# Attention followed by a SoLU feed-forward: size check, weight conversion, softmax sums and weight check placed differently

## The chip, the cores and the metric

The kernel runs on one core of a Trainium2 chip. The metric is the device time in microseconds of one execution. The times of the kernel before are 870.80, 867.64 and 868.82 us, median 868.82. Names of engines: PE is TensorE (matmuls), PEld its weight loads, DVE is VectorE, ACT is ScalarE, POOL is GpSimd, SP is the engine whose queue issues most transfers.

## The reference, cut to what matters

```python
# attention: q, k, v are (8, 12, 448, 64)
q_n, k_n = rmsnorm(q, g_q), rmsnorm(k, g_k)
scores = q_n @ k_n.T / 8
attn = exp(scores - max) / (sum(exp(scores - max)) + 1e-9)
x = attn @ v                      # then laid out as (3584 tokens, 768)
# feed-forward: w_in (768, 1024), w_out (1024, 768), given as 8-byte floats
h = x @ w_in
u = h * softmax(h)                # over the 1024 columns
ln = (u - mean(u)) / sqrt(var(u) + 1e-6) * g_ln
out = ln @ w_out                  # (3584, 768), float32
```

## The kernel before

The kernel has a fast path and a general one. The fast path computes with number ranges that it checks as it goes: the gains (`gain_limit`), the absolute size of x (`largest`), and the exponents of all weights (`check_w`, `check_all`). At the end one flag says whether the general path must run; with these inputs it doesn't. What follows is the fast path.

**Attention.** The 96 heads go two at a time as a pair `n`, and two pairs make a quad `m`, 24 quads in all. For each pair `scores` makes keys-by-queries blocks, ACT takes their exponentials (`E`, L756), and `values` multiplies them with v. The last 64 keys of both pairs of a quad are handled together (`scores_last`, `values_last`, block number `NJ` = 3). The denominators come from `sums`: matmuls with a matrix of ones over `E` 3 (of the quad), `E` 2 (of each pair), and `es`, which is `E` 0 + `E` 1, added beforehand on DVE by `add` (L789). Each of the three terms takes eight matmuls. `inverse` and `divide` finish the quad, and `store_x` writes it to a DRAM buffer.

**Weights.** Twelve pieces of w_in and sixteen of w_out arrive as raw 64-bit words and are converted by `convert_w` in three steps: `low_bits` (two ACT operations, L521 and L522), `join` (two DVE operations, L527 and L528), and, for w_out, `product` (one ACT operation, L533). Twenty pieces are converted during the quads. The last eight, all of w_out, have their loads issued when the attention's buffers are released after quad 23. `combine` then makes differences of weight blocks on POOL (L548), four for each of the four row blocks c of w_out.

**Feed-forward.** 28 token tiles go two at a time as a group `g`. Each of the two products of a group is computed with seven block products instead of eight (Strassen's scheme in Winograd's form). These need sums of the left operand's blocks, made on POOL by `block_sums`: `xsum` of x for the first product, `us` of the transposed u for the second, two operations for part 0 and two for part 1. `in_parts(g)` is the list of the seven products with w_in, in the order p1, p6, p2, p7, p5, p4, p3; `out_parts(g)` is the same with w_out. After a group's h is there, each tile t goes through `ff_max` (DVE), `ff_exp` (ACT), `ff_mult` (DVE), `ff_moments` (DVE, with a power on POOL at L999), `ff_norm` (DVE) and `ff_spread` (a DVE transpose at L1013 and sixteen small transfers into `uT` at L1020). For tile 0 half of these transfers are issued from ACT's queue.

**What sets the order.** Everything lies in a section with a schedule written by hand: on each engine the instructions run in the order in which the Python code emits them. Each entry of the list `parts` is one unit, one block product. The units are in(0), in(1), in(2), out(0), in(3), out(1) and so on, seven each, and out(12), out(13) at the end. `follow(parts, i, f)` emits f directly after unit i; `later(n, f)` emits f n units on, and things due at the same time come out in the order in which they were registered. For g = 0 and 1 the tile steps come 1, 2, 3, 4, 5 and 6 units after the product that completes h, tile 2g+1 one unit before tile 2g. So the steps of tiles 1 and 0 begin after units 5 and 6, those of tiles 3 and 2 after units 12 and 13. `block_sums` for `xsum` of group 2 come after units 9 and 10, of group 3 after 16 and 17; for `us` of group 0 after 18 and 19. The first product with w_out is unit 21; unit 22 is the first that reads `us`.

The eight late conversions, in the kernel before, are placed by this line:

```python
follow(parts, (1, 2, 2, 3, 4, 4, 5, 6)[i], lambda x=x: convert_next(x))
```

and the sixteen combines of w_out after units 0 to 3, 3 to 6, 8 to 11 and 12 to 15. `largest(g + 1)` comes after the second product of `in_parts(g)`, and for group 0 at the end of quad 22. `check_all` comes after unit 188, before the last seven products. Five PSUM buffers serve the block products, so PE may run up to five units ahead of the DVE operations that consume them (L928).

Of the kernel before, what the change touches and what calls it, by code (L numbers as in the profile page):

```python
# [366 lines left out]
def fast_path(  # L367
# [192 lines left out]
    def check_w(x, raw):  # L560
# [2 lines left out]
        nc.vector.tensor_reduce(extent[:, 0, x : x + 1], hi, AX, OP.min, apply_absolute_value=True)  # L563
        nc.vector.tensor_reduce(extent[:, 1, x : x + 1], hi, AX, OP.max, apply_absolute_value=True)

    def check_all():


        worst = small.tile([P, 3], FP32, tag="worst", name="worst", bufs=1)
        one = small.tile([1, 4], FP32, tag="one", name="one", bufs=1)  # L570
        pw = ps_t.tile([P, 4, P], FP32, tag="t", name="pw")[0:1]
        nc.vector.tensor_reduce(worst[:, 0:1], extent[:, 0], AX, OP.min)
        nc.vector.tensor_reduce(worst[:, 1:2], extent[:, 1], AX, OP.max)
        nc.vector.tensor_reduce(worst[:, 2:3], xmax, AX, OP.max)
        for i in range(3):
            nc.tensor.transpose(pw[:, i], worst[:, i : i + 1], ident)
        nc.vector.tensor_reduce(one[:, 0:1], pw[:, 0], AX, OP.min)
        nc.vector.tensor_reduce(one[:, 1:3], pw[:, 1:3], AX, OP.max)
        nc.vector.tensor_scalar(one[:, 0:1], one[:, 0:1], 2.0 ** -15, None, OP.is_ge)
        nc.vector.tensor_scalar(one[:, 1:2], one[:, 1:2], 2.0, None, OP.is_lt)  # L580
        nc.vector.tensor_scalar(one[:, 2:3], one[:, 2:3], 4.0, None, OP.is_le)
        nc.vector.tensor_tensor(one[:, 0:1], one[:, 0:1], one[:, 1:2], OP.mult)
        nc.vector.tensor_tensor(one[:, 0:1], one[:, 0:1], one[:, 2:3], OP.mult)

        nc.vector.tensor_scalar(one[:, 1:2], large, -1.0, 1.0, OP.mult, OP.add)
        nc.vector.tensor_tensor(one[:, 0:1], one[:, 0:1], one[:, 1:2], OP.mult)
        nc.vector.tensor_scalar(large, one[:, 0:1], -1.0, 1.0, OP.mult, OP.add)
# [195 lines left out]

    def add(n):
        d = st[n]
        d["es"] = work.tile([P, 2, S], FP32, tag="es", name="es")
        nc.vector.tensor_tensor(d["es"], d["E", 0], d["E", 1], OP.add)  # L789

    def values_last(m):

# [22 lines left out]
    def sums(m):  # L815

        d = quads[m]
        sm = d["sm"] = ps_t.tile([P, S], FP32, tag="t", name="sm")
        terms = [
            lambda i: (ones[:, 1 + i], d["E", NJ]),  # L820
            lambda i: (ones[:, 0], st[2 * m + i]["E", 2]),
            lambda i: (ones[:, 0], st[2 * m + i]["es"]),
        ]
        for x, term in enumerate(terms):
            for h in range(2):
                for i in range(2):
# [47 lines left out]
            (nc.sync if g < LAG else nc.scalar).dma_start(x[:, :, o : o + n], xd[b].rearrange("(c p) t -> p c t", p=P)[:, :, c : c + n])  # L874
            t += n

    def largest(g):
        nc.vector.tensor_reduce(
            xmax[:, g : g + 1], gs[g, "x"].rearrange("p c t -> p (c t)"), AX, OP.max, apply_absolute_value=True
        )  # L880

    def x_blocks(g):
        x = gs[g, "x"]
        gs[g, "s"] = xs.tile([P, 3, HD, P], FP32, tag="x", name="xsum")
        return [x[:, i * HD : (i + 1) * HD, k * P : (k + 1) * P] for k in range(2) for i in range(2)]

    def u_blocks(g):
# [17 lines left out]
    def products(g, kind, w, n, c11, c12, c21, c22, done):  # L907


        k = {}  # L910

        def mul(a, i):
            a11, a12, a21, a22 = gs[g, kind]
            sm = gs[g, "s" if kind == "A" else "us"]
            a = {"a11": a11, "a12": a12, "s3": a21, "a22": a22, "s1": sm[:, 0], "s2": sm[:, 1], "s4": sm[:, 2]}[a]
            tag = "tttoo"[len(banks) % 5]
            banks.append(tag)
            o = k["o"] = ps_t.tile([P, 512], FP32, tag=tag, name="b", bufs=3 if tag == "t" else 2)[:, 0:n]
            last = a.shape[1] - 1
            for c in range(last + 1):  # L920
                nc.tensor.matmul(o, a[:, c], w[:, i, c], start=(c == 0), stop=(c == last))  # L921

        def part(name):
            k[name] = second.tile([P, 512], FP32, tag="part", name=name, bufs=4)[:, 0:n]
            return k[name]

        def plus(out, x):
            nc.vector.tensor_tensor(out, k["o"], k[x], OP.add)  # L928

        def p1():  # L930
            mul("a11", 0)
            nc.scalar.copy(part("q1"), k["o"])  # L932

        def p6():
            mul("s2", 5)
            plus(part("u2"), "q1")

        def p2():
            mul("a12", 1)
            plus(c11(), "q1")  # L940
# [83 lines left out]
    def in_parts(g):  # L1024
        def done(i):
            t = 2 * g + i

            units = (1, 2, 3, 5, 7, 9) if g >= LAG else (1, 2, 3, 4, 5, 6)
            for x, f in zip(units, (ff_max, ff_exp, ff_mult, ff_moments, ff_norm, ff_spread)):
                later(x, lambda f=f: f(t))  # L1030

        h = [lambda t=2 * g + k, i=i: half_of(t, "h", DFF // 2, "h", i, 3) for k in range(2) for i in range(2)]
        p = products(g, "A", w_in, DFF // 2, *h, done)
        if g + 2 < NG:
            follow(p, 6, lambda: load_x(g + 2))
        if g + 1 < NG:
            follow(p, 1, lambda: largest(g + 1))
            follow(p, 2, lambda: block_sums(g + 1, "A", 0))
            follow(p, 3, lambda: block_sums(g + 1, "A", 1))
        if g >= LAG:  # L1040
            follow(p, 2 if g > LAG else 4, lambda: block_sums(g - LAG, "U", 0))
            follow(p, 4 if g > LAG else 5, lambda: block_sums(g - LAG, "U", 1))
        return p

    def out_parts(g):
        def done(i):
            t = 2 * g + i
            queue = nc.scalar if t == NT - 2 else nc.sync
            queue.dma_start(out[t * P : (t + 1) * P, :], mt.pop(t)["y"])

        y = [lambda t=2 * g + k, i=i: half_of(t, "y", HO, "y", i, 3) for k in range(2) for i in range(2)]
        p = products(g, "U", w_out, HO, *y, done)
        if NG - LAG <= g + 1 < NG:
            follow(p, 4, lambda: block_sums(g + 1, "U", 0))
            follow(p, 5, lambda: block_sums(g + 1, "U", 1))
        return p

    def follow(p, i, f):
        g = p[i]

        def both():
            g()
            later(1, f)

        p[i] = both
# [25 lines left out]
    xmax = consts.tile([P, NG], FP32, name="xmax")  # L1091
    raws = []
    sets = {}

# [23 lines left out]
    with tc.manual_schedule():  # L1118
# [4 lines left out]
        rsqrt_seed(st[0])  # L1123
        gain_columns()
        rsqrt_step(st[0])
        gain_limit()
        for s in range(2):
            normalise_rows(0, s)
            transpose_rows(0, s)
        take_rows(0, 0)  # L1130
        for s in range(2):
            square_rows(1, s, nc.scalar)
# [5 lines left out]
        for m in range(NQ):  # L1138
# [88 lines left out]
                    load(b + 6)  # L1227
            if m >= NQ // 2:
                combine(w_in, m - NQ // 2)
            unit(lambda: scores(b, 2))  # L1230
            if m == 1:
                qk_transpose(a + 2)
# [14 lines left out]
            if next2:  # L1247
                row_sums(b + 4)
                fold_sums(m + 2)
            unit(outputs)  # L1250
            step(m - 2)
            begin(m)
# [11 lines left out]
                later(1, lambda m=m: divide(m))  # L1264
            if m == NQ - 2:
                load_x(0)
                largest(0)
        divide(NQ - 1)
        store_x(NQ - 1)
        first.close()  # L1270
# [27 lines left out]
            parts += out_parts(NG - LAG + g)  # L1298

        for i, x in enumerate(left):  # L1300
            follow(parts, (1, 2, 2, 3, 4, 4, 5, 6)[i], lambda x=x: convert_next(x))
        for x in range(4 * HF):
            follow(parts, (0, 3, 8, 12)[x // 4] + x % 4, lambda x=x: combine(w_out, x))
        follow(parts, 14, check_first)

        for x in range(len(again)):
            follow(parts, (2 * LAG + 1 + 2 * (x // 3)) * 7 - 7 * LAG + (0, 4, 5)[x % 3], lambda x=x: check_next(x))
        follow(parts, 7 * (2 * NG - 1) - 1, check_all)
        for p in parts:
            unit(p)  # L1310
        for _ in range(10):
# [56 lines left out]
```

## Time and profile before

| | |
|---|---|
| median of three runs | 868.82 us |
| profiled span | 868.3 us, mean granted TensorE clock 0.993 |
| PE, DVE, ACT, POOL busy | 838.3, 653.4, 315.7, 321.0 us |
| chain that ended last | PE 77%, SP's queue 7%, DMA 4%, POOL 3%, DVE 3% |
| attention, quads 0 to 23 | up to 340.2 us |
| units of the feed-forward | from 340.2 us on |
| end of the last product, last store issued | 862.9 us, 863.5 us |

A row of the table of groups reads: line, engine, operation, output<-input by the program's names, shape, count, then busy time and mean ns of one, then the engine's idle time before them and its releaser. A row of a timeline reads: start and length in us, engine, line, operation, tiles, shape, count, and in square brackets the idle time before it with what ended it. A row of a windows table gives a stretch, its length, the busy time of each engine with the number of instructions, the granted clock, the DMA share and GB/s.

### The profile page before, as it was taken

To read this page: it belongs to the slowest core of one execution; us is meant where nothing else is said; L and a number is where in the kernel's file an instruction comes from. 1 tells how busy PE (TensorE), PEld (TensorE's weight loads), DVE (VectorE), ACT (ScalarE), POOL (GpSimd) and SP (SyncE) were. 2 spreads that over 40 slices of the span, in tenths; PEclk is the share of its full clock that TensorE was granted. 3 is DMA by queue.
4 is the path that set the end of the run, shared out by engine and by line. 5 is a ranking of instruction groups with operands and counts; after the bars stand their busy time and mean duration, and the time that the engine had idled before them with its cause. 6 is when DMAs were issued, how large, how long until landed. Compare 5 with 4: busy or idle time off the path is not lost.

```text
span 868.3 us, 12637 instructions
## 1 busy us (share of the span) xinstructions
PE 838.3 (97%) x4080; PEld 381.9 (44%) x4080; DVE 653.4 (75%) x1028; ACT 315.7 (36%) x475; POOL 321.0 (37%) x434
## 2 busy tenths in 40 slices
PE   5999999999999999986999999999999999999997
PEld 3333333333333333432554545545455454554554
DVE  5878988889999885899767768677686776755642
ACT  5677877878778772612010101101001011010100
POOL 1443453454645546365224222242222422223220
PEclk9999999999999999998999999999999999999999
DMA  6777877788777762525545355443554434222141
GB/s 125 151 154 178 199 153 183 163 190 190 148 169 146 171 163 78 163 48 135 127 97 134 84 130 134 93 109 86 135 135 97 104 85 110 69 41 62 40 105 41
DMA packets 351387, 106.94 MB, mean 123 GB/s; under 512 B 309840, under 2 KB 340560, under 8 KB 351312
## 3 DMA queue, kind: packets, MB, share of 16 engines
q1 hardware_dynamic: 332560, 95.46, 48.1%
q10 hardware_dynamic: 18752, 10.59, 4.5%
q8 instruction: 34, 0.56, 0.3%
q14 instruction: 41, 0.34, 0.1%
HBM read 69.28 MB, written 22.02 MB: 105 GB/s over the span
## 4 chain that ended last, share of the span: by engine, by line
PE 77%; SPq 7%; DMA 4%; POOL 3%; issue 3%; DVE 3%; ACT 1%; ACTq 0%; POOLq 0%; DVEq 0%
PE b L921 51%; PE o L810 9%; PE s L766 9%; PE sm L829 5%; SPq L605 4%; DMA qk<-in_k_dram 2%; SPq L504 2%; PE s L779 2%; PE o L799 1%; DMA v<-in_v_dram 1%; ACT E L756 1%; POOL w_out L548 1%; SPq L1020 0%; DVE part L635 0%; POOL ss L645 0%
## 5 line engine op out<-in xcount | busy, mean ns | idle before, releaser
L921 PE MATMUL b<-w_out,uT 128*128 128x384 f32 x448 | 152.0, 488 | 1.4 <-DMA uT<-ub 1.4
L921 PE MATMUL b<-w_in,xg 128*128 128x512 f32 x336 | 151.3, 593 | 0.6 <-DVE h L928 0.6
L756 ACT ACTIVATE E<-s 128x896 f32<-128x896 f32 x168 | 139.0, 933 | 9.2 <-PE s L766 8.8
L921 PE MATMUL b<-w_out,us 128*128 128x384 f32 x336 | 118.0, 495 | 7.1 <-POOL us L902 7.1
L766 PE MATMUL s<-qkT 64*64 64x448 f32 x1152 | 123.3, 555 | 1.1 <-DVE qkT L749 0.8
L921 PE MATMUL b<-w_in,xsum 128*128 128x512 f32 x252 | 115.1, 592 | 2.4 <-POOL xsum L902 2.4
L921 PEld LDWEIGHTS b<-w_out,uT 128*128 128x128 f32 x448 | 85.4, 191 | 64.1 <-issue 3.2
L810 PE MATMUL o<-E,v 128*64 128x448 f32 x576 | 113.5, 543 | 0.0
L999 POOL TENSOR_TENSOR he<-he,mhalf 128x1 f32<-128x1 f32 x28 | 17.2, 614 | 248.4 <-DVE he L998 248.4
L932 ACT COPY q<-b 128x512 f32<-128x512 f32 (+1 forms) x28 | 14.8, 530 | 255.2 <-PE b L921 254.9
L981 ACT ACTIVATE u<-h,hmax 128x1024 f32<-128x1024 f32 x28 | 32.2, 1149 | 190.9 <-DVE hmax L975 172.0
L921 PEld LDWEIGHTS b<-w_in,xg 128*128 128x128 f32 x336 | 63.6, 190 | 79.4 <-issue 73.7
L921 PEld LDWEIGHTS b<-w_out,us 128*128 128x128 f32 x336 | 64.8, 193 | 53.0 <-POOL us L902 7.7
L684 POOL TENSOR_TENSOR qkn<-qk,ny 128x896 f32<-128x896 f32 x46 | 77.9, 1714 | 24.9 <-DMA qk<-in_k_dram 17.7
L766 PEld LDWEIGHTS s<-qkT 64*64 64x64 f32 x1152 | 47.1, 164 | 71.0 <-ACT E L756 32.0
L645 POOL COPY ss<-part 32x56 f32<-32x56 f32 x88 | 32.9, 374 | 117.7 <-DVE part L635 115.0
L921 PEld LDWEIGHTS b<-w_in,xsum 128*128 128x128 f32 x252 | 47.8, 190 | 63.1 <-issue 59.3
L810 PEld LDWEIGHTS o<-E,v 128*64 128x64 f32 x576 | 39.2, 137 | 72.7 <-issue 64.0
L789 DVE TENSOR_TENSOR es<-E 128x896 f32<-128x896 f32 x48 | 63.9, 1333 | 0.0
L928 DVE TENSOR_TENSOR h<-b,u 128x512 f32<-128x512 f32 x42 | 28.9, 688 | 41.8 <-PE b L921 41.8
L635 DVE TENSOR_REDUCE part<-sq 128x28 f32<-128x896 f32 x46 | 49.3, 1072 | 6.9 <-ACT sq L627 6.3
L928 DVE TENSOR_TENSOR u<-b,u 128x512 f32<-128x512 f32 (+1 forms) x56 | 34.6, 619 | 26.1 <-PE b L921 24.5
(103 smaller groups left out, 1004.1 us busy)
## 6 DMA issues: line engine op xcount, KB each, us to landing
uT<-ub SPq DMA_DIRECT2D x432, 32.0 KB, 1.9
xd<-xo SPq DMA_DIRECT2D x24, 448.0 KB, 3.9
out_dram<-y SPq DMA_DIRECT2D x27, 384.0 KB, 4.3
qk<-in_q_dram SPq DMA_DIRECT2D x184, 56.0 KB, 2.4
qk<-in_k_dram SPq DMA_DIRECT2D x184, 56.0 KB, 2.2
v<-in_v_dram SPq DMA_DIRECT2D x24, 384.0 KB, 4.9
raw<-in_moe_w_in_dram SPq DMA_DIRECT2D x12, 512.0 KB, 4.8
raw<-in_moe_w_out_dram SPq DMA_DIRECT2D x64, 96.0 KB, 2.3
```

Source lines behind the costliest of these rows:

```text
L605: nc.sync.dma_start(d["qk"][g * 32 : g * 32 + 32, s], src[b, h0 + g // 2].rearrange("(b t) (x d) -> x t b d", t=32, x=2)[g % 2],)
L635: nc.vector.tensor_reduce(norms[m]["part"][:, i], st[n]["sq"], AX, OP.add)
L645: e.tensor_copy(ss[g * 32 : g * 32 + 32], part[o * 32 : o * 32 + 32])
L684: e.tensor_tensor(d["qkn"], d["qk"].rearrange("p s b d -> p (s b) d"), y.rearrange("p b -> p b ()").to_broadcast([P, 2 * NB, 32]), OP.mult,)
L756: nc.scalar.activation(d["E", kc], s[:, :, 0:S], AF.Exp)
L766: nc.tensor.matmul(s[c : c + D, h, 0:S], d["qkT"][hh, 1, keys], d["qkT"][hh, 0, :], start=True, stop=True,)
L789: nc.vector.tensor_tensor(d["es"], d["E", 0], d["E", 1], OP.add)
L810: nc.tensor.matmul(d["o"][h * D : (h + 1) * D, :], quads[n // 2]["v"][:, n % 2 * 2 + h, kc], d["E", kc][:, h], start=False, stop=(kc == NJ ...
L829: nc.tensor.matmul(sm[g : g + 32, :], w, e[:, h], start=(x == 0), stop=(x == len(terms) - 1))
L921: nc.tensor.matmul(o, a[:, c], w[:, i, c], start=(c == 0), stop=(c == last))
L928: nc.vector.tensor_tensor(out, k["o"], k[x], OP.add)
L981: nc.scalar.activation(d["u"], d["h"], AF.Exp, bias=d["nmax"], accum_out=d["s"])
```

## The change

Six edits are made.

1. The size check of x moves from a DVE reduction (largest absolute value) to two ACT operations a group (`Square` with a row sum); the limit becomes 256 for a sum of squares. The squares themselves are thrown away, into the tile that `block_sums` will later fill.
2. Of the last eight conversions three come later, after units 11 to 13.
3. Of the combines of w_out four are done in quads 22 and 23, the other twelve come after units 9 to 18.
4. In quad 22 `es` takes up `E` 2 too, in quad 23 `E` 2 and `E` 3, by DVE adds (`add_more`). The ones-matmuls for these terms are left out.
5. `check_all` is split: its reductions over partitions' rows (`check_worst`) come after unit 187, its transposes and flag after unit 189. In the start, `gain_limit` comes after the first rows are normalised and transposed.
6. The last group's outputs are stored in four halves, each as soon as it is there, instead of two whole tiles.

They are meant to take work off DVE, to let the first token tiles not wait for weights, and to shorten start and end.

```diff
-    def check_all():
-        worst = small.tile([P, 3], FP32, tag="worst", name="worst", bufs=1)
+    def check_worst():
         nc.vector.tensor_reduce(worst[:, 0:1], extent[:, 0], AX, OP.min)
         nc.vector.tensor_reduce(worst[:, 1:2], extent[:, 1], AX, OP.max)
         nc.vector.tensor_reduce(worst[:, 2:3], xmax, AX, OP.max)
+
+    def check_all():
...
-        nc.vector.tensor_scalar(one[:, 2:3], one[:, 2:3], 4.0, None, OP.is_le)
+        nc.vector.tensor_scalar(one[:, 2:3], one[:, 2:3], 256.0, None, OP.is_le)
...
+    def on_vector(m):
+        return {NQ - 2: 1, NQ - 1: 2}.get(m, 0)
...
+    def add_more(n):
+        d = st[n]
+        if on_vector(n // 2) > 0:
+            nc.vector.tensor_tensor(d["es"], d["es"], d["E", 2], OP.add)
+        if on_vector(n // 2) > 1:
+            pp = slice(n % 2 * D, n % 2 * D + D)
+            nc.vector.tensor_tensor(d["es"][pp], d["es"][pp], quads[n // 2]["E", NJ][pp], OP.add)
...
-        ]
+        ][(0, 2, 2)[on_vector(m)] :]
+        if on_vector(m) == 1:
+            terms = [lambda i: (ones[:, 1 + i], d["E", NJ])] + terms
...
-    def largest(g):
-        nc.vector.tensor_reduce(
-            xmax[:, g : g + 1], gs[g, "x"].rearrange("p c t -> p (c t)"), AX, OP.max, apply_absolute_value=True
-        )
+    def sizes(g):
+        x = gs[g, "x"].rearrange("p c t -> p (c t)")
+        n = HD * 2 * P
+        sm = gs[g, "s"] = xs.tile([P, 3, HD, P], FP32, tag="x", name="xsum")
+        for i in range(2):
+            nc.scalar.activation(
+                sm.rearrange("p k c t -> p (k c t)")[:, 0:n], x[:, i * n : (i + 1) * n], AF.Square,
+                accum_out=xmax[:, 2 * g + i : 2 * g + i + 1],
+            )
...
-            follow(p, 1, lambda: largest(g + 1))
+            follow(p, 1, lambda: sizes(g + 1))
...
-            queue = nc.scalar if t == NT - 2 else nc.sync
-            queue.dma_start(out[t * P : (t + 1) * P, :], mt.pop(t)["y"])
+            if g < NG - 1:
+                nc.sync.dma_start(out[t * P : (t + 1) * P, :], mt.pop(t)["y"])
+
+        def store(t, i, queue):
+            c = slice(i * HO, (i + 1) * HO)
+            queue.dma_start(out[t * P : (t + 1) * P, c], mt[t]["y"][:, c])
...
+        if g == NG - 1:
+            follow(p, 2, lambda: store(2 * g, 0, nc.sync))
+            follow(p, 4, lambda: store(2 * g + 1, 1, nc.sync))
+            follow(p, 5, lambda: store(2 * g + 1, 0, nc.sync))
+            follow(p, 6, lambda: store(2 * g, 1, nc.scalar))
...
-        gain_limit()
         for s in range(2):
             normalise_rows(0, s)
             transpose_rows(0, s)
+        gain_limit()
...
+            if m >= NQ - 2:
+                for i in range(2):
+                    combine(w_out, 2 * (m - NQ + 2) + i)
             unit(lambda: scores(b, 2))
...
+            add_more(a)
+            add_more(b)
             unit(outputs)
...
-            follow(parts, (1, 2, 2, 3, 4, 4, 5, 6)[i], lambda x=x: convert_next(x))
-        for x in range(4 * HF):
-            follow(parts, (0, 3, 8, 12)[x // 4] + x % 4, lambda x=x: combine(w_out, x))
+            follow(parts, (1, 1, 2, 3, 4, 11, 12, 13)[i], lambda x=x: convert_next(x))
+        for x in range(4, 4 * HF):
+            follow(parts, (9, 10, 11, 12, 13, 14, 14, 15, 16, 17, 17, 18)[x - 4], lambda x=x: combine(w_out, x))
...
-        follow(parts, 7 * (2 * NG - 1) - 1, check_all)
+        follow(parts, 7 * (2 * NG - 1) - 2, check_worst)
+        follow(parts, 7 * (2 * NG - 1), check_all)
```

More of the change, by code (lines that the diff above doesn't have):

```diff
@@ L564, in check_w @@
         nc.vector.tensor_reduce(extent[:, 1, x : x + 1], hi, AX, OP.max, apply_absolute_value=True)
-    def check_all():
-        worst = small.tile([P, 3], FP32, tag="worst", name="worst", bufs=1)
-        one = small.tile([1, 4], FP32, tag="one", name="one", bufs=1)
-        pw = ps_t.tile([P, 4, P], FP32, tag="t", name="pw")[0:1]
+    def check_worst():
         nc.vector.tensor_reduce(worst[:, 0:1], extent[:, 0], AX, OP.min)
@@ L574, in check_all @@
         nc.vector.tensor_reduce(worst[:, 2:3], xmax, AX, OP.max)
+    def check_all():
+        one = small.tile([1, 4], FP32, tag="one", name="one", bufs=1)
+        pw = ps_t.tile([P, 4, P], FP32, tag="t", name="pw")[0:1]
         for i in range(3):
@@ L875, in load_x @@
             t += n
-    def largest(g):
-        nc.vector.tensor_reduce(
-            xmax[:, g : g + 1], gs[g, "x"].rearrange("p c t -> p (c t)"), AX, OP.max, apply_absolute_value=True
-        )
+    def sizes(g):
[7 more added lines that the diff above has]
+            )
     def x_blocks(g):
         x = gs[g, "x"]
-        gs[g, "s"] = xs.tile([P, 3, HD, P], FP32, tag="x", name="xsum")
         return [x[:, i * HD : (i + 1) * HD, k * P : (k + 1) * P] for k in range(2) for i in range(2)]
@@ L1090, in fast_path @@
     extent = consts.tile([P, 2, len(again)], FP32, name="extent")
-    xmax = consts.tile([P, NG], FP32, name="xmax")
+    xmax = consts.tile([P, 2 * NG], FP32, name="xmax")
+    worst = consts.tile([P, 3], FP32, name="worst")
     raws = []
@@ L1266, in fast_path @@
                 load_x(0)
-                largest(0)
+                sizes(0)
         divide(NQ - 1)
```

## The prediction, made before the changed kernel ran

> **What bounds the kernel now.** First the page's engine line and the windows of the middle of the span:
>
> ```profile
> PE 838.3 (97%) x4080; PEld 381.9 (44%) x4080; DVE 653.4 (75%) x1028; ACT 315.7 (36%) x475; POOL 321.0 (37%) x434
> ...
> 370.00:380.00 10.00, 9.37 (x22) 3.65 (x20) 9.76 (x21) 1.29 (x3) 2.70 (x3) 1.00 0.02 6
> 380.00:390.00 10.00, 7.61 (x18) 3.53 (x19) 8.85 (x10) 0.00 (x0) 9.69 (x11) 1.00 0.32 53
> 390.00:400.00 10.00, 8.84 (x21) 3.63 (x20) 7.95 (x13) 2.96 (x5) 3.23 (x3) 1.00 0.71 142
> 400.00:410.00 10.00, 2.87 (x8) 1.45 (x7) 9.83 (x16) 0.90 (x1) 8.09 (x8) 0.76 0.36 108
> 410.00:420.00 10.00, 10.00 (x24) 5.60 (x23) 7.63 (x12) 1.95 (x5) 1.72 (x2) 0.72 0.58 127
> ```
>
> The columns are PE, PEld, DVE, ACT, POOL busy, then granted clock. TensorE has no slack elsewhere; it falls idle only between 376 and 409 us, where the attention has ended and the first output product begins. The timeline of PE gives each hole with its releaser:
>
> ```profile
> 377.10 2.84 PE L921 MATMUL b<-w_in,xg 128*128 128x512 f32 x6 [0.57 <-DVE h L928]
> 382.39 2.84 PE L921 MATMUL b<-w_in,xsum 128*128 128x512 f32 x6 [2.45 <-POOL xsum L902]
> ...
> 399.37 2.82 PE L921 MATMUL b<-w_out,uT 128*128 128x384 f32 x8 [1.16 <-DMA uT<-ub]
> 409.32 5.49 PE L921 MATMUL b<-w_out,us 128*128 128x384 f32 x8 [7.13 <-POOL us L902]
> ```
>
> Together 11.3 us. From 409.32 PE runs without a hole to 843, so the start of that product (number 22, counting from 0 at 340.21) sets the end. I therefore follow what releases it:
>
> ```profile
> 364.96 1.21 DVE L975 TENSOR_REDUCE hmax<-h 128x1 f32<-128x1024 f32 x1
> ...
> 384.00 1.23 DVE L1013 STREAM_TRANSPOSE ub<-u 128x1024 f32<-128x1024 f32 x1
> 385.27 5.36 ACTq L1020 DMA_DIRECT2D uT<-ub  x8
> ...
> 390.67 1.15 ACT L981 ACTIVATE u<-h,hmax 128x1024 f32<-128x1024 f32 x1 [18.87 <-DMA uT<-ub]
> ...
> 401.76 0.55 POOL L999 TENSOR_TENSOR he<-he,mhalf 128x1 f32<-128x1 f32 x1 [3.59 <-DVE he L998]
> 402.27 0.99 POOL L901 TENSOR_TENSOR xsum<-xg 128x384 f32<-128x384 f32 x1
> ...
> 406.66 1.26 POOL L901 TENSOR_TENSOR us<-uT 128x512 f32<-128x512 f32 x1
> 408.00 1.26 POOL L902 TENSOR_TENSOR us<-us,uT 128x512 f32<-128x512 f32 x1
> ```
>
> Read: DVE starts token tile 1's hmax late, behind the joins of weight pieces whose loads are still landing; at 385.23 tile 0 is transposed and ACT is held for 5.36 us issuing eight of its transfers; only then can ACT take the exponentials of tiles 3 and 2; their moments on DVE release `he` of tile 2 at 401.76, and behind it POOL, in program order, does four xsum operations, then the us that PE needs.
>
> **What the skill says.** The Trainium skill, TensorE: Matmul & The Clock Gate, Part 1: The HAM clock gate, says a TensorE idle for about 3.4 us drops to half clock. The trace agrees: after 7.13 us idle the product took 5.49 us instead of about 2.6, after 2.45 us it didn't. The 25 matmuls from 409.32 end at 420.39; warm they'd need 25 x 0.322 = 8.05 plus 0.17, so the drop costs 2.9 us. The same page, Architectural detail, calls ACT and DVE strict FIFO: ACT's 18.87 us wait above shows it. GPSIMD Engine Reference, Key points: GpSimd shares its SBUF interfaces with DVE instructions having two SBUF inputs. Agreed: the L789 add takes 1.04 us at least and 2.19 at most.
>
> **The change, part by part.**
>
> *Size check.* Removes fourteen L878 reductions of 1.743 us (24.4 us of DVE), adds 28 Squares of 128x768 on ACT. Rows of Square: 0.63 us at 512 columns, 0.975 at 896, so about 0.86, plus an accumulator read of 0.19 (L981's): 2.1 us a group. After 409 this is worth nothing: DVE has slack and PE is full. In the middle it removes 1.75 us from DVE at 349.5, 374.7 and 396.72. On ACT the first lies in the idle 4.5 us before 327.97 (its load was issued at 318.62, and such loads take 4.8). POOL's xsum now waits for the Square, which uses that tile as scratch: xsum(1) moves from 344.5 to about 350.6, needed by PE at 360.8. Free.
>
> *Sums on DVE.* Removes 8 ones-matmuls in quad 22 and 16 in quad 23: 24 x 0.1 = 2.4 us of PE. Adds six adds; rows of L789 bound each: 1.04 alone, 1.5 beside POOL (3.05 for two at 332.12). Quad 22: es of b ends 323.2, the two adds 325.4; PE wants es at 325.2. Saves 0.6. Quad 23: the divides end about 331.3, then es twice and four more adds at 1.04 to 1.5: 339.4 to 340.3, with the new w_out combines and xsum on POOL beside them. PE would be ready at 337.2 and now waits 2 to 3 us for es before its last 8 matmuls (0.8 us). They end at 340.2 to 341.1, before at 340.21. Gain and wait cancel: I take 0 (-1.0 to +0.9). Whatever it is, it shifts the last xo store and the weight loads behind it (SP issues from 348.14).
>
> *Conversions.* Of eight pieces five keep units near the old ones, three go to after units 11 to 13. ACT's first read of a piece is at 351.70, the loads arrive 1.85 us apart, so piece 4 lands at 359.1; ACT's two operations 1.2, DVE's join 1.13: 362.1. hmax of tile 1 now follows directly, at 362.1 instead of 364.96. From there DVE is gapless: hmax 1.15, h 0.6, hmax 1.15, multiply 1.15, u 0.6, moments 2.0, multiply 1.15, h 0.6, norm 0.75, moments 2.0, u 0.6, transpose 1.24, norm 0.8, two adds 1.25, transpose 1.24 = 16.3, plus 0.3 of contention: tile 0 is transposed at **378.7** instead of 385.23, 6.5 us earlier. That closes the 0.57 and 2.45 holes.
>
> Then comes the new wait. ACT issues its eight transfers until 384.1 (378.7 + 5.4). The first late piece is queued behind them on ACT, and its join stands ahead of hmax of tile 3 on DVE, by the unit numbers. DVE, idle from about 379.6, waits until 385.3. After that, counted from 384.1: first ACT half 1.25, join 1.13, hmax 1.15, h 0.6, join 1.1, hmax 1.15, multiply 1.15, join 1.1, u 0.6, moments 2.0, multiply 1.15, h 0.6, norm 0.7, moments 2.0 = 15.7. Before, the same stretch took 401.70 - 390.63 = 11.1, with one L878 in it. So `he` of tile 2 is ready at **399.8**, only 1.9 us earlier.
>
> *Combines.* Four go into quads 22 and 23, twelve to after units 9 to 18. Unit 16 puts one between the xsum pair, units 17 put two more ahead of us. POOL took 7.56 us from `he` to us (401.76 to 409.32); with three more at 0.99 it takes 10.6 (up to 11.9 at the contended 1.45). Us is done at **410.4** against 409.3: +1.1. PE's product 21 is by then long done, so its hole is some 10 us and the half clock is paid again, at the same 2.9 us.
>
> *Start.* Three DVE operations (7.80 to 8.50) leave PE's path: at most 0.7. The chain there is SP issuing loads back to back to 31.58, so I take 0.
>
> *End.* Before, the three transposes at 843.86 lay in a hole whose last releaser was the uT transfer landing at 844.5; now they stand after product 189, on PE's path: 0.3. DVE's 4.5 us of flag arithmetic delays u, which has 10 us to spare. The last store is 192 KB instead of 384 (3.2 us on that queue). A 192 KB xg load takes 3.1, a 96 KB raw 2.3: saves 0.1 to 0.9, I take 0.6. Sum -0.3.
>
> Total 868.8 + 1.1 - 0.3 = **869.6 us**.
>
> **Rivals.**
> *A, faster.* The late join doesn't hold DVE, or its load is off the path, and POOL meets us with its combines done. Then `he` comes 6 us earlier than before at equal POOL time: 868.8 - 6.0 - 0.3 = 862.5. At best all holes go: product 22 at 340.2 + 22 x 2.575 = 396.9, 12.5 earlier, no half clock (2.9): 853. For it: DVE sheds 24 us, and tile 0 is indeed earlier. Against: ACT's order above.
> *B, slower.* Contention is at its upper end throughout: quad 23 +0.9, three joins at 2.0 instead of 1.1 (rows of 1.25 plus 0.75 at 352.94) +2.7, combines +1.3, L902 at its median 1.6, +0.3: 869.6 + 5.2 = 874.8. For it: POOL works at 380 to 386 and after 396, as DVE does. Against: the late joins mostly meet an idle POOL.
>
> **How the numbers follow.** Forecast 0.50, A 0.27, B 0.23. Half a per cent is 4.3 us, so the forecast is "same" (864.5 to 873.2). The range reaches to half of A's span and past B: 858 to 876; outside lie the hole-free end of A and a slower B, together some 0.15.
>
> **What would show it.** Tile 0's transpose near 378.7; a DVE wait of about 5 us on ACT's low bits near 380; `he` of tile 2 near 400; three w_out combines between it and us; product 22 near 410 and again slow; an es wait near 337. Wrong, if product 22 starts before 406 or after 413, or if PE shows holes after it.

## The result, and the profile after

The changed kernel takes 877.07 us (median of 4 executions, 876.17 to 879.5), the kernel before 869.39 beside it: a recorded ratio of 1.0094 (the two medians alone would give 1.0088), interval 1.0065 to 1.0123. **It is slower by 0.9%**, where 869.6 us and "no change" were forecast; the time lies 1 us above the range.

The two profiles, cut at the starts of the products that the prediction used (differences of rows of the PE timelines):

| stretch | before | after | difference |
|---|---|---|---|
| start to the first matmul of quad 23 | 326.82 | 327.35 | +0.5 |
| quad 23 to product 0 | 13.39 | 15.63 | +2.2 |
| product 0 to product 22 | 69.11 | 71.04 | +1.9 |
| product 22 to the end of the span | 459.0 | 460.9 | +1.9 |
| span | 868.3 | 874.9 | +6.6 |

First the engine line of the page after, and its windows of the middle, to be laid beside those of before (columns as there: PE, PEld, DVE, ACT, POOL busy, granted clock, DMA share, GB/s):

```profile
PE 838.1 (96%) x4056; PEld 381.7 (44%) x4056; DVE 628.6 (72%) x1020; ACT 341.5 (39%) x531; POOL 318.7 (36%) x434
...
370.00:380.00 10.00, 10.00 (x25) 4.42 (x24) 9.79 (x20) 1.87 (x4) 5.90 (x6) 1.00 0.05 9
380.00:390.00 10.00, 10.00 (x25) 4.50 (x24) 3.79 (x6) 2.86 (x5) 7.30 (x8) 1.00 0.49 74
390.00:400.00 10.00, 9.70 (x23) 4.11 (x23) 9.83 (x18) 6.96 (x13) 2.42 (x2) 1.00 0.78 193
400.00:410.00 10.00, 2.14 (x7) 0.95 (x5) 9.86 (x16) 0.12 (x1) 7.32 (x9) 0.72 0.15 23
410.00:420.00 10.00, 5.98 (x13) 3.35 (x14) 4.89 (x7) 2.73 (x5) 7.28 (x6) 0.60 0.60 126
```

DVE is rid of 24.8 us in all, as meant. PE is full from 370 to 399, where it had holes before. But DVE, which worked 8.85 us of the ten from 380 on before, now works 3.79, and PE pays after 400: 2.14 busy us instead of 2.87, then 5.98 instead of 10.00. The PE timeline shows the holes that are left, with their releasers:

```profile
338.58 0.91 PE L844 MATMUL sm<-es,ones 128*32 128x448 f32 x2 [0.29 <-DVE es L802]
342.09 0.95 PE L844 MATMUL sm<-es,ones 128*32 128x448 f32 x6 [2.60 <-DVE es L802]
...
399.29 2.85 PE L941 MATMUL b<-w_out,uT 128*128 128x384 f32 x8 [0.30 <-DVE h L948]
414.02 4.84 PE L941 MATMUL b<-w_out,us 128*128 128x384 f32 x8 [11.88 <-POOL us L922]
...
844.01 2.74 PE L941 MATMUL b<-w_out,us 128*128 128x384 f32 x8
849.64 2.82 PE L941 MATMUL b<-w_out,uT 128*128 128x384 f32 x8 [2.89 <-DMA uT<-ub]
852.30 0.49 PE L577 MATMUL pw<-ident,worst 128*1 128x128 f32 x3
```

The early holes of 0.57, 2.45 and 1.16 us have all but gone, and the one before product 22 has grown from 7.13 to 11.88 us: gathered in one place, with more added. The two waits on `es` are new. The other engines' rows give the chain to product 22, in the order of the prediction (timelines of DVE, ACT and POOL, put together by time; rows left out at the dots):

```profile
364.37 1.21 DVE L995 TENSOR_REDUCE hmax<-h 128x1 f32<-128x1024 f32 x1
...
379.76 1.23 DVE L1033 STREAM_TRANSPOSE ub<-u 128x1024 f32<-128x1024 f32 x1
381.02 5.37 ACTq L1040 DMA_DIRECT2D uT<-ub  x8
386.50 0.66 ACT L521 ACTIVATE tmp<-raw,seven 128x384 f32<-128x384 uint32 x1 [13.92 <-DMA uT<-ub]
...
387.75 0.56 DVE L527 SCALAR_TENSOR_TENSOR tmp<-raw,tmp 128x384 uint32<-128x384 uint32 x1 [6.18 <-ACT tmp L522]
...
402.53 0.56 POOL L1019 TENSOR_TENSOR he<-he,mhalf 128x1 f32<-128x1 f32 x1 [2.52 <-DVE he L1018]
...
405.08 1.44 POOL L548 TENSOR_TENSOR w_out<-w_out 128x384 f32<-128x384 f32 x1
...
408.40 2.07 POOL L548 TENSOR_TENSOR w_out<-w_out 128x384 f32<-128x384 f32 x2
410.43 1.27 POOL L921 TENSOR_TENSOR us<-uT 128x512 f32<-128x512 f32 x1
411.77 2.19 POOL L922 TENSOR_TENSOR us<-us,uT 128x512 f32<-128x512 f32 x1
```

These rows show the new wait whole. DVE transposes tile 0 at 379.76, 4.2 us earlier than before (7.0 counted from product 0); ACT is then held 5.37 us by eight issues, the first late conversion comes out of ACT at 387.71, and DVE, whose next instruction is the join, has waited 6.18 us for it. That ACT's transfers cause this wait is tested below. `he` of tile 2 then comes at 402.53 (before 401.76), and POOL has three combines between it and `us`.

### The profile page after: what moved, and what is told of

It is laid out like the page before. It is cut to its first block, busy times and chain, and to the rows that moved or that the text cites. A ratio compares the mean times of both kernels' runs of the same rounds, so it can differ in the third digit from the quotient of the medians.

```text
span 874.9 us, 12613 instructions
## 1 busy us (share of the span) xinstructions
PE 838.1 (96%) x4056; PEld 381.7 (44%) x4056; DVE 628.6 (72%) x1020; ACT 341.5 (39%) x531; POOL 318.7 (36%) x434
## 4 chain that ended last, share of the span: by engine, by line
PE 49%; DVE 4%; SPq 2%; POOL 1%; issue 1%; DMA 1%; ACTq 1%; ACT 0%; DVEq 0%; POOLq 0%
PE b L941 49%; SPq L1040 2%; DVE hmax L995 1%; DVE tmp L527 1%; ACTq L1040 1%; DVE u L948 0%; DVE h L948 0%; DVE bs L1013 0%; POOL w_out L548 0%; DVE u L1005 0%; DMA xd<-xo 0%; DVE ub L1033 0%; DMA out_dram<-y 0%; DVE u L1023 0%; DMA raw<-in_moe_w_out_dram 0%
## 5 line engine op out<-in xcount | busy, mean ns | idle before, releaser
L941 PE MATMUL b<-w_out,us 128*128 128x384 f32 x336 | 117.3, 493 | 11.9 <-POOL us L922 11.9
L685 POOL TENSOR_TENSOR qkn<-qk,ny 128x896 f32<-128x896 f32 x46 | 78.0, 1715 | 22.7 <-DMA qk<-in_q_dram 11.9
L948 DVE TENSOR_TENSOR u<-b,q 128x512 f32<-128x512 f32 (+1 forms) x28 | 17.5, 624 | 51.8 <-PE b L941 48.2
```

Source lines behind the costliest of these rows:

```text
L685: e.tensor_tensor(d["qkn"], d["qk"].rearrange("p s b d -> p (s b) d"), y.rearrange("p b -> p b ()").to_broadcast([P, 2 * NB, 32]), OP.mult,)
```

## Experiments

Each ratio is to executions of the kernel before on the same chip; the quantities read in the profile are the distances from the first matmul of quad 23 to product 0 and from there to product 22, since the attention differs in length between executions (last experiment). In the four profiles where nothing in the middle was altered the latter is 71.04 to 71.06; in the two profiles of the kernel before it is 69.1 and 69.4, so differences of half a microsecond and more are read.

| kernel | us | ratio (interval) | quad 23 to product 0 | product 0 to 22 |
|---|---|---|---|---|
| changed, again | 880.76 | 1.0101 (1.0077 to 1.0126) | 15.6 | 71.0 |
| changed, sums on PE | 874.65 | 1.0036 (1.0022 to 1.0050) | 13.3 | 71.1 |
| changed, old places of conversions and combines | 872.21 | 1.0005 (0.9989 to 1.0020) | 14.1 | 67.8 |
| changed, whole stores | 878.5 | 1.0078 (1.0052 to 1.0103) | 15.6 | 71.1 |
| changed, size check on DVE | 880.76 | 1.0110 (1.0082 to 1.0139) | 15.8 | 73.5 |
| changed, combines not ahead of us | 876.13 | 1.0043 (1.0025 to 1.0062) | 15.6 | 68.0 |
| changed, ACT halves early | 875.41 | 1.0033 (1.0019 to 1.0047) | 15.8 | 66.9 |
| reordered | 866.63 | 0.9938 (0.9915 to 0.9961) | 13.3 | 58.3 |
| reordered, weight checks later | 861.5 | 0.9883 (0.9860 to 0.9907) | 13.3 | 57.7 |
| before, size check on ACT | 872.13 | 0.9996 (0.9978 to 1.0013) | 13.3 | 67.9 |
| before, us first | 864.26 | 0.9916 (0.9893 to 0.9938) | 13.4 | 63.1 |

**The sums of exponentials.** The adds on DVE are undone; the ones-matmuls come back.

```diff
-        return {NQ - 2: 1, NQ - 1: 2}.get(m, 0)
+        return 0
```

> The changed kernel with its fourth edit undone: no further adds into es in the last two quads, the ones-matmuls are back. In the changed kernel the four adds of quad 23 took 7.3 us beside POOL and PE waited 2.6 us for the last of them, so the last sums ended at 342.9 instead of about 340.4. Theory (this wait is handed on through the last xo store, the weight loads and DVE to the first us product): the last sums end 2.4 us earlier and product 22 starts 2.4 us earlier, time near 877.1 - 2.5 = 874.6, 1.0060 of before. Rival (the wait is hidden, since PE is ahead of what releases product 22): time stays at 877, 1.009 of before, although the sums end earlier.

Measured: 874.65 us, 1.0036, against 1.0078 and 1.0101 of the kernels with the adds. In its PE timeline the `es` waits are gone, and all eight ones-matmuls run together:

```profile
342.47 0.94 PE L844 MATMUL sm<-es,ones 128*32 128x448 f32 x8
...
414.40 4.47 PE L941 MATMUL b<-w_out,us 128*128 128x384 f32 x8 [11.88 <-POOL us L922]
```

Quad 23 to product 0 is back at 13.26 us, and the middle is untouched (71.06). So **the adds cost 2.4 us there**. The time fell by more, 3.9 us beside the kernel with whole stores on the same chip; part lies in the end of the span (hole before the last group's product 1.65 instead of 2.89, last store 5.4 us from issue to end instead of 6.0), where the edit has no part; the rest isn't located. The DVE rows after the change show why the adds cost so much, with POOL's beside them:

```profile
334.75 1.88 DVE L799 TENSOR_TENSOR es<-es,E 128x896 f32<-128x896 f32 x1
336.67 1.77 DVE L802 TENSOR_TENSOR es<-es,E 64x896 f32<-64x896 f32 x1
338.36 1.88 DVE L799 TENSOR_TENSOR es<-es,E 128x896 f32<-128x896 f32 x1
340.27 1.77 DVE L802 TENSOR_TENSOR es<-es,E 64x896 f32<-64x896 f32 x1
```

```profile
330.84 3.04 POOL L548 TENSOR_TENSOR w_out<-w_out 128x384 f32<-128x384 f32 x2
333.84 1.84 POOL L921 TENSOR_TENSOR xsum<-xg 128x384 f32<-128x384 f32 x1
335.76 1.73 POOL L922 TENSOR_TENSOR xsum<-xsum,xg 128x384 f32<-128x384 f32 x1
337.46 1.84 POOL L924 TENSOR_TENSOR xg<-xg 128x384 f32<-128x384 f32 x1
339.26 1.84 POOL L925 TENSOR_TENSOR xsum<-xg,xsum 128x384 f32<-128x384 f32 x1
```

All four meet a working POOL and take 1.77 to 1.88 us, and POOL's adds 1.73 to 1.84 instead of 0.99: the two engines slow each other down alike. On both, one add starts 1.7 to 1.9 us after the other, not far from 1.08 and 0.99 added up, as if they took turns. The last of them ends at 342.04, and PE waits for it.

The same is seen in quad 22, where the change leaves out eight ones-matmuls:

```profile
320.60 3.86 POOL L548 TENSOR_TENSOR w_out<-w_out 128x384 f32<-128x384 f32 x2
323.52 2.90 DVE L799 TENSOR_TENSOR es<-es,E 128x896 f32<-128x896 f32 x2
325.55 1.87 PE L844 MATMUL sm<-es,ones 128*32 128x448 f32 x8
```

The eight matmuls with `es` take 1.87 us instead of 0.94, and quad 22 lasts 13.55 us. Before it lasted 13.37, and 13.26 to 13.61 in all profiles without the adds, so nothing is saved there.

**Conversions and combines in their old places.**

```diff
-            if m >= NQ - 2:
-                for i in range(2):
-                    combine(w_out, 2 * (m - NQ + 2) + i)
...
-            follow(parts, (1, 1, 2, 3, 4, 11, 12, 13)[i], ...)
+            follow(parts, (1, 2, 2, 3, 4, 4, 5, 6)[i], ...)
-        for x in range(4, 4 * HF):
-            follow(parts, (9, 10, 11, 12, 13, 14, 14, 15, 16, 17, 17, 18)[x - 4], ...)
+        for x in range(4 * HF):
+            follow(parts, (0, 3, 8, 12)[x // 4] + x % 4, ...)
```

> The changed kernel with its second and third edits undone: the eight late conversions and the sixteen combines of w_out are placed as in the kernel before. Theory (the join that waits behind ACT's transfers, and the three combines ahead of us on POOL, are what costs): he of tile 2 is 3 to 5 us earlier than at 402.5, POOL takes 7.6 us from it to us instead of 11.4, product 22 starts near 409 to 410 in spite of the late sums, time near 873, 1.004 of before. Rival (the late sums cost it all, the places are neutral): time stays at 877, product 22 at 414.

Measured: 872.21 us, 1.0005: almost all of the loss is gone. Product 0 to 22 is 67.76, 3.3 us less, and `he` to product 22 is 7.57 us again, as before. It also takes part of the adds' cost away, which had not been foreseen; its DVE rows:

```profile
337.21 1.77 DVE L802 TENSOR_TENSOR es<-es,E 64x896 f32<-64x896 f32 x1
338.90 1.08 DVE L799 TENSOR_TENSOR es<-es,E 128x896 f32<-128x896 f32 x1
340.02 1.09 DVE L802 TENSOR_TENSOR es<-es,E 64x896 f32<-64x896 f32 x1
```

Without the two combines in quad 23, POOL ends its xsum at 338.03 instead of 341.10, and the last two adds run alone: 1.08 and 1.09. The wait before the last ones-matmuls is 1.12 instead of 2.60. Quad 22 shortens to 12.74 us. From the start of quad 22 to product 0 it is 26.88 us here with the adds alone, 26.55 in the preceding experiment with the early combines alone, 26.76 in the kernel before, and 29.18 with both: **adds and early combines cost next to nothing apart, and 2.4 us together.**

**Whole stores at the end.**

```diff
-            if g < NG - 1:
-                nc.sync.dma_start(out[t * P : (t + 1) * P, :], mt.pop(t)["y"])
+            queue = nc.scalar if t == NT - 2 else nc.sync
+            queue.dma_start(out[t * P : (t + 1) * P, :], mt.pop(t)["y"])
...   (the four half stores are taken out)
```

> The changed kernel with its sixth edit undone: the last two tiles are stored whole. In the profiles the time from the issue of the last store to the end of the span was 4.8 us before and 6.0 us after. Theory (four half stores end later than two whole ones): time near 876, 1.2 us less, and 4.8 us from last issue to end. Rival (my prediction: halves save 0.6 us): 877.7. Second rival (the 1.2 us belongs to something else at the end): still 6.0 us from last issue to end, time unchanged.

Measured: 878.5 us, 1.0078, beside 1.0101 of the unaltered change. From the issue of the last store to the end of the span it is 5.6 us with the whole tile and 6.0 with half of one; over all runs 4.8 to 5.6 whole and 4.6 to 6.0 halved. **Halving the stores saves nothing** that can be seen.

**Size check on DVE.** In the changed kernel the two Squares of a group are replaced by the reduction of before.

```diff
-            nc.scalar.activation(sm..., x[:, i * n : (i + 1) * n], AF.Square, accum_out=...)
+        nc.vector.tensor_reduce(xmax[:, g : g + 1], x, AX, OP.max, apply_absolute_value=True)
```

> The changed kernel with its first edit undone: the size check of x is a DVE reduction again (limit 4 on the largest absolute value). Theory (DVE is the gapless engine between 364 and 403, so two reductions of 1.75 us lie on the path to product 22): product 22 about 3.5 us later than 414, time near 880.5, 1.013 of before. Rival (DVE waits for ACT's low bits for 6 us anyway, which hides the first of the two): 1.75 us later, 878.8. Second rival (no effect): 877.

Measured: 880.76 us, 1.0110. Product 0 to 22 is 73.5, 2.5 more than with the Squares; the intervals of the times overlap, so the reading rests on the profile:

```profile
392.90 2.84 PE L939 MATMUL b<-w_in,xsum 128*128 128x512 f32 x6 [2.48 <-DVE h L946]
...
417.33 5.19 PE L939 MATMUL b<-w_out,us 128*128 128x384 f32 x8 [11.28 <-POOL us L920]
```

Where the change's product stream runs on until 399 us, a hole on DVE's `h` is there at 392.90, and the long one stays. The size check on ACT is thus the one edit of those tested that helps the middle, and the others outweigh it.

**The two causes in the middle, one at a time.** First the combines that stood between `he` and `us` go ahead of `he` in POOL's order:

```diff
-            follow(parts, (9, 10, 11, 12, 13, 14, 14, 15, 16, 17, 17, 18)[x - 4], ...)
+            follow(parts, (9, 10, 11, 12, 13, 14, 14, 14, 15, 15, 15, 18)[x - 4], ...)
```

> The changed kernel with only the last combines of w_out moved: the three that stood between he of tile 2 and us on POOL now come after unit 15, ahead of that he, where POOL waits anyway (units 9, 10, 11, 12, 13, 14, 14, 14, 15, 15, 15, 18). Theory (POOL's queue ahead of us is on the path): from he of tile 2 to product 22 it takes 7.6 to 8.3 us instead of 11.4, product 22 comes 66.8 to 68 us after product 0 instead of 71.0, time 3 to 4 us less than the changed kernel on the same chip. Rival (POOL would wait there anyway, for a load or for DVE): no change, 71 us.

Then, instead, ACT's halves of the three late conversions are issued early, ahead of the eight transfers, and the joins stay in their units:

```diff
-            follow(parts, (1, 1, 2, 3, 4, 11, 12, 13)[i], ...)
+            follow(parts, (1, 1, 2, 3, 4, 8, 9, 10)[i], ...)   # for the last three: join 4 units on, product 5
```

> The changed kernel with only the ACT halves of the three late conversions moved: they follow units 8 to 10, ahead of ACT's eight transfers for tile 0, and the DVE joins stay where the change put them. Theory (the join that waits behind ACT's transfers holds DVE for 6.2 us, and with it the moments of tiles 3 and 2): the 6.2 us wait is gone, he of tile 2 comes about 5 us earlier, product 22 comes 66 us after product 0 instead of 71.0, time 5 us less than the changed kernel on the same chip. Rival (the exponentials of tiles 3 and 2 wait behind the same transfers and end last anyway): at most 2.5 us.

> The changed kernel itself once more, on the same chip as its variants. All theories: 1.008 to 1.010 of before, product 22 about 71 us after product 0, against 69.1 before.

Measured: 876.13, 875.41 and 880.76 us. The long hole in the PE timelines of the first and the second:

```profile
413.74 4.94 PE L941 MATMUL b<-w_out,us 128*128 128x384 f32 x8 [8.01 <-POOL us L922]
```

```profile
413.79 5.40 PE L941 MATMUL b<-w_out,us 128*128 128x384 f32 x8 [8.32 <-POOL us L922]
```

Against 71.04 of the change, 68.0 (3.0 less) and 66.9 (4.1 less). Both causes are real: ACT's transfers ahead of the conversions, and POOL's combines ahead of `us`. In the first run `he` of tile 2 to product 22 takes 7.57 us instead of 11.49, though `he` itself comes 0.9 later, now behind the combines; in the second DVE's wait of 6.18 us is gone and `he` comes 4.1 us earlier, counted from product 0. Expected were 66.8 to 68 and 66. In neither has the hole closed; POOL's remaining order, four xsum operations before `us`, is what the next runs change.

**Reordered.** Both edits together (the joins here 3 units after ACT's halves, one unit earlier than in the change), the sums on PE, and `us` of the first tiles put ahead of xsum on POOL:

```diff
-            follow(p, 2 if g > LAG else 4, lambda: block_sums(g - LAG, "U", 0))
-            follow(p, 4 if g > LAG else 5, lambda: block_sums(g - LAG, "U", 1))
+            follow(p, 2 if g > LAG else 1, lambda: block_sums(g - LAG, "U", 0))
+            follow(p, 4 if g > LAG else 2, lambda: block_sums(g - LAG, "U", 1))
...
+            follow(parts, (9, 10, 11, 11, 12, 12, 13, 13, 14, 14, 14, 17)[x - 4], ...)
```

> The changed kernel with four places altered: no further adds into es (edit 4 undone), the ACT halves of the late conversions after units 8 to 10 and their joins one unit earlier, all combines but one ahead of he of tile 3, and the first us sums of group 0 ahead of the xsum sums of group 3 on POOL (after units 15 and 16 instead of 18 and 19). Theory (the three queues are the whole of the hole before product 22): product 22 comes 56.6 to 58 us after product 0, there is no half clock, time about 12.5 + 2.5 us less than before plus 0.3 for the transposes at the end: 855 where before is 869, ratio 0.983 to 0.986. Rival (the eight transfers and their landing hold it): product 22 not before 61 us after product 0, with a hole and a half clock, ratio 0.990 to 0.995.

Measured: 866.63 us, 0.9938. The middle fell to 58.3 us, but some of the gain was given back further on (timelines of PE, SP's queue and DVE, put together):

```profile
400.99 2.82 PE L941 MATMUL b<-w_out,us 128*128 128x384 f32 x8 [1.33 <-POOL he L1019]
...
402.02 23.56 SPq L1040 DMA_DIRECT2D uT<-ub  x32
...
430.30 0.62 DVE L563 TENSOR_REDUCE extent<-again 128x1 f32<-128x448 f32 x1 [8.41 <-DMA again<-in_moe_w_in_dram]
431.97 4.43 PE L941 MATMUL b<-w_in,xsum 128*128 128x512 f32 x6 [3.78 <-DVE y L948]
```

The loads of the weight check are queued on SP behind 32 transfers that take 23.56 us to issue. With product 22 coming 12.7 us earlier than in the change, DVE reaches the check before its load has landed and waits 8.41 us, with `y` behind it, for which PE waits.

**Weight checks later.** As the last, with the check's DVE operations, and the loads that follow each of them, fourteen units on: `(0, 4, 5)` becomes `(14, 18, 19)`.

> The reordered kernel (no further adds into es, ACT halves early, combines early, us ahead of xsum), with the checks of the weights placed two units of a group later (14 block products). In the reordered kernel DVE waited 8.4 us near 430 for a weight load of the check that stood behind 32 transfers of uT in SP's queue, PE stood for 3.8 us and then ran a product at half clock. Theory (that wait is all that is left of it): no hole between product 22 and the last output group, 5.5 us less than the reordered kernel, 0.9938 - 0.0063 = 0.9875 of before. Rival (the wait moves to the next check): 0.994.

Measured: 861.5 us, **0.9883** (0.9860 to 0.9907): faster than both kernels. Its PE timeline has two holes of under a microsecond in this stage, and product 22 runs at full clock:

```profile
401.21 2.82 PE L941 MATMUL b<-w_out,us 128*128 128x384 f32 x8 [0.77 <-POOL he L1019]
404.95 5.43 PE L941 MATMUL b<-w_out,uT 128*128 128x384 f32 x16 [0.92 <-DVE u L948]
```

**The kernel before with the size check alone on ACT.** Edit 1 by itself:

> The kernel before with only the first edit made: the size check of x on ACT. Theory (DVE is the gapless engine ahead of product 22, two of the reductions lie on its path): product 22 comes 65.6 us after product 0 instead of 69.1, time 3.5 us less, 0.996 of before. Rival (DVE waits for ACT's transfers anyway): 67.4 us and 0.998. Second rival (no effect): 69.1 and 1.000.

Measured: 872.13 us, 0.9996. The middle is 67.9, some 1.4 us less than the 69.1 and 69.4 of before, and the time doesn't show it:

```profile
384.34 5.49 PE L925 MATMUL b<-w_in,xsum 128*128 128x512 f32 x6 [3.07 <-POOL xsum L906]
...
410.26 4.54 PE L925 MATMUL b<-w_out,us 128*128 128x384 f32 x8 [4.55 <-POOL us L906]
```

The hole before product 22 shrank from 7.1 to 4.55, but part of that is only PE coming to it later: the wait on xsum grew to 3.07, and the product after it ran at half clock, 5.49 us. A lighter DVE alone is worth little here.

**The kernel before with us first** (the two `follow` lines above, and the checks fourteen units on; nothing else):

> The kernel before with the first us sums placed ahead of the xsum sums of group 3 (after units 15 and 16 instead of 18 and 19), and the checks of the weights 14 block products later. Theory (what held product 22 was POOL's order, not the data, which had landed by 399.7): product 22 comes 62.5 us after product 0 instead of 69.1, without half clock, time 7 + 2.9 us less, 0.9886 of before. Rival (he of tile 2, now behind us on POOL, delays tile 2 and a later product stands instead): 0.994 to 1.000.

Measured: 864.26 us, 0.9916, somewhat less than expected; the hole before product 22 is nearly closed with every other row of before in place:

```profile
405.17 2.82 PE L921 MATMUL b<-w_out,us 128*128 128x384 f32 x8 [0.40 <-POOL he L999]
```

The 7.13 us that the prediction set out from were thus mainly POOL's order, not the lateness of `he`. It gains 8.6 us on the kernel before, the reordered kernel with later checks 11.4 on the same chip: most of that gain needs none of the six edits. Whether it needs the later checks was not tried.

**The kernel before, profiled once more.**

> The kernel before, profiled once more. In its first profile the scores of quad 23 began at 326.8 us, in nine profiles of the changed kernel and its variants at 327.0 to 331.1. If the attention is as long in both kernels, this profile lies at 327 to 331 too, with product 22 again 69.1 us after product 0; if the change makes the attention longer, it lies at 326.8.

Measured: quad 23 starts at 331.88, in the first profile of the same kernel at 326.82; product 0 to 22 is 69.4 against 69.1. The attention's length differs by 5 us with nothing changed, so a time read from the span's start is not comparable between two profiles, a distance inside is. Its PE timeline also shows how unsteady the half clock is:

```profile
331.88 2.52 PE L766 MATMUL s<-qkT 64*64 64x448 f32 x24
...
387.47 4.34 PE L921 MATMUL b<-w_in,xsum 128*128 128x512 f32 x6 [2.45 <-POOL xsum L902]
...
414.68 4.39 PE L921 MATMUL b<-w_out,us 128*128 128x384 f32 x8 [7.09 <-POOL us L902]
```

The same 2.45 us hole was followed by 2.84 us in the first profile. The recorded clock of these ten microseconds (380 to 390) is 0.86 here and 1.00 there.

## Why the prediction was wrong

Its chain and its order of events in the middle held; the sum failed by the size of a few terms. It forecast +0.8 us, and the profile is +6.6: 0.5 lies in the attention before quad 23, where one kernel differs by 5 us between executions, 2.2 in the sums of quad 23, 0.8 in the middle beyond the +1.1 forecast, and 2.2 in the end beyond the -0.3.

- **"Sums on DVE", "I take 0": failed, the largest step that a run ties to an edit.** Its own terms have the last sums end 0 to 0.9 us later than before, so the 0 was the lower end. The adds were given 1.04 to 1.5 us, though the prediction had read a row of 2.19; those of quad 23 took 1.77 to 1.88. That the new combines lie beside them was said, but not priced. The wait of "2 to 3 us" came (0.29 and 2.60), but the eight matmuls behind it ran as two and six and took 0.91 and 0.95 us, not 0.8 in all, and the 0.6 us of quad 22 were not saved. Measured +2.2 in quad 23, +2.4 with quad 22, 2.4 by undoing the adds, and next to nothing (+0.1) where the combines were taken away instead.
- **Tile 0's transpose at 378.7, `he` of tile 2 at 399.8: right** as distances. Product 0 came 2.8 us later than assumed (342.98 instead of 340.2). Counted from it, the transpose ended after 38.0 us (38.5 predicted), ACT was free after 43.4 (43.9), `he` began after 59.6 (59.6). The new DVE wait, about 5 us, was 6.18. The half microsecond comes from the first step: hmax of tile 1 was put at 362.1, 21.9 us after product 0, where its terms (359.1, 1.2 and 1.13) give 361.4; it came after 21.4.
- **"With three more at 0.99 it takes 10.6 (up to 11.9)": its value was 0.9 short, its range held.** `he` to product 22 took 11.5, nearly all of the excess in L922, 2.19 us instead of 1.26. The three combines were there as named; one took 1.44, and the xsum operation after it 0.99 instead of the 1.45 of before.
- **The middle as a whole:** 410.4 - 340.2 = 70.2 was predicted, 71.04 measured. The middle was wrong by 0.8 only. Taking parts of it out gave 3.0 and 4.1 us, so the mechanism is shown.
- **Half clock "paid again, at the same 2.9 us": too high by 1.1.** From product 22 on, the first 24 matmuls took 9.83 us, before 10.91, and 9.39 in the second profile of before. It varies by 1.5 us in one and the same kernel. (The rows that the sum counted as 25 matmuls hold 24; by its own figures the drop cost 3.2 us, not 2.9.)
- **End, "Sum -0.3": failed, with the sign.** After product 22 the profile gained 1.9 us: 0.33 for the transposes, on PE's path as said (852.30 to 852.63); 1.5 in the step from the product before to the last group's first one, 5.63 us (844.01 to 849.64) where it was 4.17 with the transposes inside; 1.2 in the last store, whose saving of 0.6 doesn't exist; less 1.1 of half clock. The rows of before:

```profile
840.38 2.74 PE L921 MATMUL b<-w_out,us 128*128 128x384 f32 x8
843.86 0.49 PE L576 MATMUL pw<-ident,worst 128*1 128x128 f32 x3 [0.74 <-DVE worst L572]
844.55 2.85 PE L921 MATMUL b<-w_out,uT 128*128 128x384 f32 x8 [0.20 <-DMA uT<-ub]
```

  The store is scatter (4.6 to 6.0). That step may be more than scatter: it is 4.12 to 4.51 us in the four profiles with the old end and 4.39 to 5.63 in the ten with the new one, with medians 4.15 and 4.76. No run that undoes one of the other edits brings it back to 4.2; the fifth, the split check, was not undone alone, and why PE waits longer for `uT` there stays open.
- **Start at 0:** right. PE's first transposes came at 8.71 instead of 9.24, and at the start of quad 3 the lead was gone (58.08 against 57.95).
- **Size check: nothing "After 409", something in the middle:** right, 2.5 us by the run that put it back; on the kernel before alone 1.4 in the profile, too little for the interval of its time (0.9978 to 1.0013) to show or exclude.
- **The choice of case.** Rival B, contention at its upper end, gave 874.8 and had 0.23. It is nearest, in part by luck: of its +5.2 the +2.7 for the joins did not come, and terms that it didn't have filled the place. But contention was on the rows: POOL works from 330.8 to 341.1 without a break beside DVE's adds. What spoke against it concerned only the late joins, which did meet an idle POOL (the first took 1.06 us, 387.75 to 388.81, not 2.0); the argument was carried over to the adds without a look at POOL's load beside them. B's own term for them, +0.9, was too small as well, by 1.3 of the +2.2 measured, so the range built on B ended at 876, 1 us short.
- **Rival A, "POOL meets us with its combines done", 862.5 at once and 853 at best:** not what the change does, but what its parts can do. The reordered kernel with later checks, 861.5, is A with ACT's and POOL's order put right by hand and the sums back on PE.

The Trainium skill, GPSIMD Engine Reference, Key points, had been cited for the shared interfaces; the runs agree, and add the size: 1.08 us alone and 1.88 beside POOL for one and the same add. The Trainium skill, TensorE: Matmul & The Clock Gate, Part 1: The HAM clock gate, calls the window of activity free-running and its effect variable from run to run. The prediction used only its figure of about 3.4 us; here 2.45 and 3.07 us of idle PE were followed by products at 4.34 and 5.49 us, and 2.45 in another execution by 2.84. Of the 18.87 us by which the prediction showed ACT's strict order, only the last 3.6 lie behind the transfers: the `hmax` that ACT needed ended at 387.06, and ACT was free at 390.63.

## What to carry to other kernels

When work is moved to relieve one engine, read on each in-order engine what the moved instruction stands behind in its new place (here eight DMA issues on ACT) and what it stands before (here `us` on POOL): that order was worth more (8.6 us for `us` first) than the 25 us of DVE work saved (2.5 at most). Price a two-input DVE add by what POOL does in that very stretch of the changed kernel: two edits that cost nothing apart can cost 2.4 us together. And when a hole is closed, look at what was hidden in it: here a load behind 32 DMA issues, which took back part of the gain until its reader was moved.

## What the runs showed of the hardware that was not expected

- A DVE add on 64 partitions takes as long as one on 128 (1.77 and 1.88 us beside POOL, 1.09 and 1.08 alone).
- DVE and POOL slow each other alike in these adds: DVE from 1.08 to 1.88 us, POOL from 0.99 to 1.84.
- TensorE's clock can drop after an idle time of 2.45 us, and does not always: 4.34 and 2.84 us for the same product after the same hole, at recorded clocks of 0.86 and 1.00.
- The attention of one and the same kernel took 326.8 us in one execution and 331.9 in another, up to quad 23.
